# A Fourier mixing kernel rewritten: d folded at its centre, 32-row inverse tiles, PSUM bank by bank, the exchange in two ways

## The chip, the cores and the metric

One core of one Trainium2 chip. The metric is device time in microseconds (us) of one execution. The executions of one kernel spread here over about 3%, so each run is given as a median with its range, and a run that is 1.5% above the fastest of its kernel counts as "slow" and is left out of the ratios. Every ratio below is the mean time of one kernel's fast runs over that of the kernel before's fast runs in the same rounds, so it is not quite the ratio of the medians beside it. Where two variants are compared, the means of their fast runs are used; the changed kernel's is 153.7 us.

## The reference, cut to what matters

```python
g = sigmoid((x * gate_w).sum(-1, keepdims=True))      # x: (1, 2048, 1024) bf16
a = irfft2(rfft2(x) * (A_w_r + 1j * A_w_i))           # over (2048, 1024), fp32, then bf16
b = irfft2(rfft2(x) * (B_w_r + 1j * B_w_i))
return g * a + (1 - g) * b
```

The transforms are matmuls with cosine and sine tables. The 2048 rows are split as 16 x 128: F1 transforms over 128, F2 over d, F3 over the remaining 16 with the twiddles; then come the products with the weights A and B; then the inverse: I1 (16), I2 (128, with the gate folded into its table), I3 (d). The frequencies make sixteen "units", eight even and eight odd. Each unit's I1 output, 128 partitions by 2048 bf16 (0.52 MB), has to change places before I2: what lies across partitions must lie along a row. This is the *exchange*, from the tile `rl` to the row tiles `Re` (even) and `Ro` (odd), which are 32 KB per partition each. I2 of a half can't start before all eight units of the half have been exchanged.

## The kernel before

```python
    pp = ctx.enter_context(tc.tile_pool(name="pp", bufs=3, space=bass.MemoryType.PSUM))   # three buffers of two banks
    ...
    def i1(n, r):
        ...
        if r == 0:
            RLs[n] = wk.tile([P, 2, 2, 512], BF16, name="rl", tag="rl", bufs=4)
        rl = RLs[n]
        nc.scalar.copy(out=rl[:, :, r, :], in_=ps[:].rearrange("p (t m) -> p t m", t=2))
        if r == 1:
            for tt in range(2):
                t = 2 * u + tt
                p0 = 32 * (t // 4) + t % 4
                nc.gpsimd.dma_start(RR[par][p0:p0 + 29:4, :, :], rl[:, tt].rearrange("p r m -> p (r m)"))
    ...
    for n in range(12):
        f2(n)
        ...
        if n >= 3:
            i1(n - 3, 0)
        if n >= 1:
            f3(n - 1)
        if n >= 3:
            i1(n - 3, 1)
        if n >= 1:
            cmul(n - 1)          # two products and two sums on VectorE
        if n == 2:
            gate_z()
```

Two transfers of 256 KB per unit go through the GpSimd queue.

Of the kernel before, what the change touches and what calls it, by code (L numbers as in the profile page):

```python
# [20 lines left out]
WID = (257, 256)  # L21
PIT = (258, 256)
# [25 lines left out]

def make_constants():
# [3 lines left out]
    E = np.zeros((NT, 2, 2, 2, 128))  # L53
    EZ = np.zeros((NT, 2, 2, 2, 128))
    for t in range(NT):
        for j, k2 in enumerate(quad_reps(t)):
            th = 2 * np.pi * s2 * k2 / 128
            F[:, t, j // 2, 0, j % 2] = np.cos(th)
            F[:, t, j // 2, 1, j % 2] = -np.sin(th)
            E[t, j // 2, 0, j % 2] = np.cos(th)  # L60
            E[t, j // 2, 1, j % 2] = np.sin(th)
            EZ[t, j // 2, 0, j % 2] = 2 * np.cos(th)
            EZ[t, j // 2, 1, j % 2] = -2 * np.sin(th)
            if k2 == 0:
                F[:, t, j // 2, 1, j % 2] = np.cos(np.pi * s2)
                E[t, j // 2, 1, j % 2] = np.cos(np.pi * s2)
                EZ[t, j // 2, 0, j % 2] = 1
                EZ[t, j // 2, 1, j % 2] = np.cos(np.pi * s2)
    F = F.reshape(128, 128)
    c["F1"] = _bf16np(np.concatenate([F, -F], axis=1))  # L70
    c["E"] = _bf16np(E.reshape(4, 4, 8, 128).transpose(0, 2, 1, 3).reshape(128, 128))
    c["EZ"] = _bf16np(EZ.reshape(128, 128) / 128)
    d1 = np.arange(512)
    i = np.arange(256)
    FD = np.zeros((512, 2, 2, 256))
    IG = np.zeros((2, 2, 256, 512))
    for eo in range(2):
        m = 2 * i + eo
        ph = 2 * np.pi * np.outer(d1, m) / D
        FD[:, eo, 0] = np.cos(ph)  # L80
        IG[eo, 0] = 2 * np.cos(ph).T
        if eo == 0:
            IG[0, 0, 0] = 1
        m = 2 * i + (2 if eo == 0 else 1)
        ph = 2 * np.pi * np.outer(d1, m) / D
        FD[:, eo, 1] = -np.sin(ph)
        IG[eo, 1] = -2 * np.sin(ph).T
        if eo == 0:
            FD[:, 0, 1, 255] = np.cos(np.pi * d1)
            IG[0, 1, 255] = np.cos(np.pi * d1)  # L90
    IG /= S * D
    c["FD"] = _bf16np(FD.reshape(4, 128, 2, 512).transpose(1, 2, 0, 3))
    c["IG"] = _bf16np(IG.reshape(2, 2, 2, 128, 512).transpose(3, 0, 1, 2, 4).reshape(128, 8, 512))
    s1 = np.arange(NS1)
    WF = np.zeros((128, NT, 3, 64))
    WI = np.zeros((128, NT, 3, 64))
    for t in range(NT):
        for jh in range(2):
# [4 lines left out]
            for p in range(64):  # L103
                w = np.exp(-2j * np.pi * k[p] * s1 / S)
                kk = k[p] % 128
                if kk in (0, 64):
                    cc = 0 if kk == 0 else 1
                    al[:, cc, 0, p] = w
                    be[cc, 0, :, p] = w.conj()
                    continue  # L110
                eps = 1 if kk in reps else -1
                j = reps.index(kk if eps > 0 else 128 - kk)
                al[:, 0, j, p] = w
                al[:, 1, j, p] = 1j * eps * w
                be[0, j, :, p] = w.conj()
                be[1, j, :, p] = 1j * eps * w.conj()
            al = al.reshape(64, 64)
            be = be.reshape(64, 64).T
            h = slice(64 * jh, 64 * jh + 64)
            WF[h, t, 0], WF[h, t, 1], WF[h, t, 2] = al.real, al.imag, -al.imag  # L120
            h = h if t % 2 == 0 else slice(64 - 64 * jh, 128 - 64 * jh)
            WI[h, t, 0], WI[h, t, 1], WI[h, t, 2] = be.real, be.imag, -be.imag
    c["WF"] = _bf16np(WF)
    c["WI"] = _bf16np(WI)
# [4 lines left out]
def gated_mix(ctx, tc, x_in, we_in, wo_in, gw_in, out):  # L129
# [3 lines left out]
    xv = x_in.flatten_outer_dims().rearrange("(s2 s1) d -> s2 s1 d", s1=NS1)  # L133
# [5 lines left out]
    wp = ctx.enter_context(tc.tile_pool(name="wp", bufs=1))  # L139
    wk = ctx.enter_context(tc.tile_pool(name="wk", bufs=2))  # L140
    pp = ctx.enter_context(tc.tile_pool(name="pp", bufs=3, space=bass.MemoryType.PSUM))
    pl_pool = tc.alloc_tile_pool(name="plp", bufs=1, space=bass.MemoryType.PSUM)
# [4 lines left out]
    def ptile():  # L147
        return pp.tile([P, 1024], F32, name="pt", tag="pt")

    ctx.enter_context(tc.manual_schedule())  # L150
    warm = const.tile([P, 512], BF16, name="warm")
    nc.vector.memset(warm[:], 0.0)
    wps = ptile()
    for _ in range(6):
        nc.tensor.matmul(wps[:, 0:512], lhsT=warm[:, 0:128], rhs=warm[:], start=True, stop=True)  # L155
    F1 = const.tile([P, 2, 128], BF16, name="f1")
    nc.scalar.dma_start(F1[:].rearrange("p a b -> p (a b)"), dr["F1"])
    gws = const.tile([P, 8], BF16, name="gws")
    nc.scalar.dma_start(gws[:], gw_in)
    Re = big.tile([P, 16 * 1024], BF16, name="re")  # L160
    Ro = big.tile([P, 16 * 1024], BF16, name="ro")
    x = Re[:].rearrange("p (s d) -> p s d", s=NS1)
    for s0, n in ((0, 1), (1, 1), (2, 2), (4, 2), (6, 2), (8, 2), (10, 2), (12, 2), (14, 2)):
        nc.sync.dma_start(x[:, s0:s0 + n, :], xv[:, s0:s0 + n, :])
    FD = const.tile([P, 2, 4, 512], BF16, name="fd")
    WF = const.tile([P, NT, 3, 64], BF16, name="wf")
    WI = const.tile([P, NT, 3, 64], BF16, name="wi")
    IG = const.tile([P, 8, 512], BF16, name="ig")
    Ec = const.tile([P, 128], BF16, name="ec")
    Ez = const.tile([P, 128], BF16, name="ez")  # L170

    y = big.tile([P, 4, 2, 2 * NT, NS1, 4], BF16, name="y")
    Ws = {}
    wt = [wp.tile([P, 2064], BF16, name=f"w{k}", tag=f"w{k}") for k in range(4)]

    def load_w(n):
        par, u = n // NU, n % NU
        if n < 4 or 8 <= n < 12:
            w = wt[n % 4][:]
        elif n < 8:  # L180
            w = Ro[:, (n - 4) * 2064:(n - 3) * 2064]
        else:
            w = y[:, n - 12, 0].rearrange("p t s c -> p (t s c)")
        w = w[:, 0:8 * PIT[par]].rearrange("p (t a m) -> p t a m", t=2, a=4)
        nc.sync.dma_start(w, w_in[par][u])
        Ws[n] = w

    nc.sync.dma_start(FD[:, 0], dr["FD"][:, 0])
    nc.sync.dma_start(WF[:, 0:4], dr["WF"][:, 0:4])
    load_w(0)  # L190
    nc.sync.dma_start(Ez[:], dr["EZ"])
    nc.sync.dma_start(WI[:, 0:4], dr["WI"][:, 0:4])
    load_w(1)
    nc.sync.dma_start(WF[:, 4:16], dr["WF"][:, 4:16])
    load_w(2)
    nc.sync.dma_start(WI[:, 4:16], dr["WI"][:, 4:16])
    nc.sync.dma_start(Ec[:], dr["E"])
    for n in range(3, 8):
        load_w(n)
    nc.sync.dma_start(FD[:, 1], dr["FD"][:, 1])  # L200
    nc.sync.dma_start(IG[:], dr["IG"])

    gwz = const.tile([P, 8, 32], BF16, name="gwz")
    nc.gpsimd.memset(gwz[:], 0.0)
    gh = const.tile([P, 8], F32, name="gh")
    junk = const.tile([P, 8], F32, name="junk")
    nc.scalar.activation(junk[:], gwz[:, 0, 0:8], ACT.Sigmoid)
    nc.vector.tensor_scalar(gh[:], gws[:], 0.5, None, ALU.mult)
    gq = gwz[:].rearrange("p (q e) c -> p q e c", e=2)
    nc.vector.tensor_tensor(gq[:, :, 0, 0], gh[:, 0:4], gh[:, 4:8], ALU.add)  # L210
    nc.vector.tensor_tensor(gq[:, :, 1, 0], gh[:, 0:4], gh[:, 4:8], ALU.subtract)

    yo = y[:].rearrange("p q e t s c -> p (q e t) s c")
    for s1 in range(NS1):
        ps = ptile()
        for q in range(4):
            for h in range(2):
                nc.tensor.matmul(ps[:, q * 256:(q + 1) * 256],  # L218
                                 lhsT=x[:, s1, h * 512 + q * 128:h * 512 + (q + 1) * 128],
                                 rhs=(bc(F1[:, 0, :]).to_broadcast([P, 2, 128]) if h == 0 else F1[:]), start=(h == 0), stop=(h == 1))  # L220
        i_ = ps[:].rearrange("p (a c) -> p a c", c=4)
        if s1 == 15:
            for e, cp in ((0, nc.scalar.copy), (1, nc.vector.tensor_copy)):
                cp(out=y[:, :, e, :, s1, :], in_=ps[:].rearrange("p (q e t c) -> p q e t c", q=4, e=2, c=4)[:, :, e])
        elif s1 % 2 == 1:
            nc.vector.tensor_copy(out=yo[:, :, s1, :], in_=i_)  # L226
        else:
            nc.scalar.copy(out=yo[:, :, s1, :], in_=i_)  # L228

    RR = [r[:].rearrange("p (s f) -> p s f", s=NS1) for r in (Re, Ro)]  # L230
    EV = Re[:].bitcast(F32).rearrange("p (s f) -> p s f", s=NS1)
    EA = const.tile([P, NS1, 128], BF16, name="ea")
    EB = const.tile([P, NS1, 128], BF16, name="eb")
    zt = const.tile([P, NS1], BF16, name="zt")

    def gate_hat():
        ps = ptile()
        for e in range(2):
            for q in range(4):
# [154 lines left out]
    for n in range(12):  # L394
        f2(n)
        if n == 0:
            gate_hat()
# [89 lines left out]
```

## Time and profile before

146.2 us median (144.8 to 148.8); its profile spans 144.4 us. The span falls into five stretches: to the first F2 matmul, to the first product, to the first I2 of the even half, to the first I2 of the odd half, to the end. These are two, from a table of stretches of the kernel before (us from and to; length; busy time of each engine with its instructions; granted clock; DMA share; GB/s):

```profile
core 0: us, PE busy (x) PEld busy (x) DVE busy (x) ACT busy (x) POOL busy (x), PEclk, DMA share, GB/s
...
29.60:76.60 47.00, 38.21 (x427) 18.16 (x433) 42.28 (x54) 40.80 (x44) 10.81 (x18) 0.93 0.81 221
76.60:114.90 38.30, 34.22 (x346) 18.25 (x353) 24.01 (x30) 28.77 (x31) 8.29 (x14) 1.00 0.41 103
```

The transfers of the exchange, from the part on DMA issues (KB each, median us from issue to landing):

```profile
re<-rl POOLq DMA_DIRECT2D x16, 256.0 KB, 8.0
ro<-rl POOLq DMA_DIRECT2D x16, 256.0 KB, 5.1
```

### The profile page before, as it was taken

The numbers are of one execution on the slowest core, as the hardware profiler recorded it, in microseconds if no ns is written. First come the engines' busy times: TensorE is split into PE (matmuls) and PEld (weight loads), VectorE is DVE, ScalarE is ACT, GpSimd is POOL, SyncE is SP. The second block draws the span as 40 slices with busy tenths as digits, with TensorE's granted clock in tenths as the row PEclk, the third lists the DMA queues.
The fourth block names the chain that finished last, engine by engine and source line by source line (L and its number), as shares of the span: only waits on it lengthen the run. The fifth ranks groups of instructions, "written<-read, shape, count | busy, mean of one in ns | idle before, by whom it ended". The sixth has DMA issues, their size and how long they took to land.

```text
span 144.4 us, 2878 instructions
## 1 busy us (share of the span) xinstructions
PE 121.9 (84%) x1188; PEld 68.1 (47%) x1206; DVE 97.6 (68%) x113; ACT 93.3 (65%) x97; POOL 19.6 (14%) x37
## 2 busy tenths in 40 slices
PE   6999979929899898888867999868869999999910
PEld 2688844416344443334324345433455665756500
DVE  0177740089279999999999279599433456898990
ACT  4255546665699999999995899997935244253200
POOL 1000000000033222233333033033330000000000
PEclk9999999975799999999999999999999999999985
DMA  4999999968716999999865315527464000464553
GB/s 148 298 361 419 406 411 405 415 244 284 297 14 168 240 279 278 353 250 202 163 139 133 126 18 140 131 43 168 110 166 110 0 0 0 167 253 166 208 228 145
DMA packets 11088, 29.19 MB, mean 202 GB/s; under 512 B 3781, under 2 KB 4165, under 8 KB 10949
## 3 DMA queue, kind: packets, MB, share of 16 engines
q1 hardware_dynamic: 6048, 20.55, 38.3%
q0 software_dynamic: 4608, 8.41, 24.8%
q8 instruction: 9, 0.15, 0.5%
q10 hardware_dynamic: 420, 0.07, 0.3%
q14 instruction: 3, 0.02, 0.0%
HBM read 16.42 MB, written 4.19 MB: 143 GB/s over the span
## 4 chain that ended last, share of the span: by engine, by line
PE 55%; ACT 24%; DMA 9%; issue 4%; DVE 2%; another core or an unknown queue 2%; DVEq 1%; POOL 0%; ACTq 0%; POOLq 0%
PE pt L378 18%; PE pt L218 10%; PE pt L275 10%; ACT rl L349 10%; PE pv L367 9%; DMA re<-rl 5%; DMA zt<-zs 4%; ACT X L310 4%; ACT T L279 3%; PE pt L344 3%; ACT V L370 2%; PE pt L155 2%; ACT zs L245 2%; DVE ot L390 2%
## 5 line engine op out<-in xcount | busy, mean ns | idle before, releaser
L275 PE MATMUL pt<-fd,y 128*128 128x512 bf16 x117 | 30.5, 394 | 3.8 <-ACT rl L349 2.6
L349 ACT CAST rl<-pt 128x1024 bf16<-128x1024 f32 x32 | 32.9, 1038 | 0.0
L378 PE MATMUL pt<-ig,V 128*128 128x512 bf16 x121 | 29.6, 379 | 1.1 <-ACT V L370 0.7
L370 ACT CAST V<-pv 128x1024 bf16<-128x1024 f32 x16 | 16.3, 1021 | 19.2 <-PE pv L367 19.2
L344 PE MATMUL pt<-Y,wi 64*64 64x512 bf16 x256 | 20.1, 387 | 3.8 <-ACT T L279 0.8
L275 PEld LDWEIGHTS <-y 128*128 128x128 bf16 x128 | 12.6, 100 | 20.3 <-issue 8.6
L279 ACT CAST T<-pt 128x1024 bf16<-128x1024 f32 x16 | 16.3, 1017 | 8.3 <-PE pt L275 4.1
L378 PEld LDWEIGHTS <-V 128*128 128x128 bf16 x128 | 11.7, 98 | 13.9 <-ACT V L370 1.9
L354 POOL DMA_DIRECT2D re<-rl x16 | 9.6, 606 | 59.8 <-ACT rl L349 59.8
L310 ACT CAST X<-pt 128x1024 bf16<-128x1024 f32 x16 | 16.5, 1033 | 0.0
L218 PE MATMUL pt<-f_84,re 128*128 128x256 bf16 x128 | 15.6, 289 | 0.0
L218 PEld LDWEIGHTS <-re 128*128 128x128 bf16 x128 | 13.0, 103 | 3.1 <-DMA re<-in_x_dram 0.8
L228 ACT CAST y<-pt 128x1024 bf16<-128x1024 f32 x8 | 8.1, 1013 | 8.4 <-PE pt L218 8.4
L354 POOL DMA_DIRECT2D ro<-rl x16 | 9.5, 596 | 26.4 <-ACT rl L349 26.4
L386 DVE COPY re<-pt 128x1024 f32<-128x1024 f32 x5 | 6.1, 1225 | 10.2 <-PE pt L378 10.2
L226 DVE CAST y<-pt 128x1024 bf16<-128x1024 f32 x7 | 8.6, 1225 | 5.2 <-PE pt L218 5.2
L344 PEld LDWEIGHTS <-wi 64*64 64x64 bf16 x256 | 6.4, 106 | 11.9 <-issue 10.7
L389 DVE TENSOR_TENSOR ot<-pt,re 128x1024 bf16<-128x1024 f32 x8 | 9.8, 1224 | 3.0 <-PE pt L378 3.0
L367 PE MATMUL pv<-ea,re 128*128 128x128 bf16 x64 | 8.1, 219 | 2.9 <-DMA re<-rl 1.7
L295 PE MATMUL pt<-T,wf 64*64 64x512 bf16 (+2 forms) x192 | 9.8, 307 | 0.4 <-ACT T L279 0.3
L367 PEld LDWEIGHTS <-re 128*128 128x128 bf16 x128 | 7.5, 98 | 5.4 <-issue 2.5
L390 DVE TENSOR_TENSOR ot<-re,pt 128x1024 bf16<-128x1024 f32 x8 | 9.7, 1210 | 0.0
(96 smaller groups left out, 128.2 us busy)
## 6 DMA issues: line engine op xcount, KB each, us to landing
re<-rl POOLq DMA_DIRECT2D x16, 256.0 KB, 8.0
ro<-rl POOLq DMA_DIRECT2D x16, 256.0 KB, 5.1
out_dram<-ot SPq DMA_DIRECT2D x8, 512.0 KB, 2.6
re<-in_x_dram SPq DMA_DIRECT2D x7, 512.0 KB, 8.6
ro<-in_we_dram SPq DMA_DIRECT2D x4, 516.0 KB, 8.0
y<-in_wo_dram SPq DMA_DIRECT2D x4, 512.0 KB, 6.5
fd<-cst_fd SPq DMA_DIRECT2D x2, 512.0 KB, 9.1
ig<-cst_ig SPq DMA_DIRECT2D x1, 1024.0 KB
```

The costliest lines, as they stand in the source:

```text
L218: nc.tensor.matmul(ps[:, q * 256:(q + 1) * 256], lhsT=x[:, s1, h * 512 + q * 128:h * 512 + (q + 1) * 128], rhs=(bc(F1[:, 0, :]).to_broadca ...
L275: nc.tensor.matmul(ps[:, tt * 512:(tt + 1) * 512], lhsT=y[:, q, par, 2 * t:2 * t + 2, :, :].rearrange("p j s c -> p (j s c)"), rhs=FD[:, p ...
L279: nc.scalar.copy(out=T[:].rearrange("p a b -> p (a b)"), in_=ps[:])
L295: nc.tensor.matmul(ps[ho, tt * 512 + dst:tt * 512 + dst + ln], lhsT=WF[hp(jh), 2 * u + tt, w, :], rhs=T[hp(jh), tt, src:src + ln], start=( ...
L310: nc.scalar.copy(out=xo, in_=ps[:].rearrange("p (t r m) -> p t r m", t=2, r=2))
L344: nc.tensor.matmul(ps[hp(jh), tt * 512:(tt + 1) * 512], lhsT=WI[hin, 2 * u + tt, w, :], rhs=Y[hin, k, 2 * tt:2 * tt + 2, o:o + 256], start ...
L349: nc.scalar.copy(out=rl[:, :, r, :], in_=ps[:].rearrange("p (t m) -> p t m", t=2))
L354: nc.gpsimd.dma_start(RR[par][p0:p0 + 29:4, :, :], rl[:, tt].rearrange("p r m -> p (r m)"))
L367: nc.tensor.matmul(ps[:, s * 512 + ch * 128:s * 512 + ch * 128 + 128], lhsT=RR[par][:, s1, c0 + 256 * ab:c0 + 256 * ab + 128], rhs=Ew[:, s ...
L370: nc.scalar.copy(out=V[:].rearrange("p s c k -> p (s c k)"), in_=ps[:])
L378: nc.tensor.matmul(ps[:, s * 512:(s + 1) * 512], lhsT=V[:, s, ch, :], rhs=IG[:, par * 4 + ch, :], start=(ch == 0), stop=(ch == 3))
L390: nc.vector.tensor_tensor(ot[:, :, 1, :], ev, pv, ALU.subtract)
```

## The change

Its intent: less work on TensorE and VectorE, PSUM given out bank by bank instead of in three buffers of two, every instruction placed by a list. Folding d at its half-sample centre halves F2 and part of I3; I1 multiplies the products directly in 32-row tiles, so VectorE's sums go; units 0, 2, 4, ... are exchanged by the GpSimd queue, units 1, 3, 5, ... by a store to DRAM and a reload on the sync queue. The diff of some 1,000 lines, cut to its core:

```diff
+ORDER = """
+warm:6 c:A:F1 c:A:gws tab:A x:S:0:1 x:S:1:1 ...
+F2:5:0:0 P:2:0 N:0:P ... HS:1:S J:0:4:6
+W:S:6 T:4:0:A T:5:1:A W:S:7 ... c:S:IG ... HL:1:S ... H:2:0:P ...
+"""                                 # (cut: 537 entries in all)
-    pp = ctx.enter_context(tc.tile_pool(name="pp", bufs=3, space=bass.MemoryType.PSUM))
+    pp = ctx.enter_context(tc.tile_pool(name="pp", bufs=1, space=bass.MemoryType.PSUM))
+    psum = pp.tile([P, 4096], F32, name="ps")
+def exchange_row(t, i):
+    u = t // 2
+    return 64 * (u // 4) + 32 * (t % 2) + 16 * (i % 2) + 4 * (i // 2) + u % 4
-            for q in range(4):       # F2: four matmuls of 512 columns
-                nc.tensor.matmul(ps[:, tt * 512:(tt + 1) * 512], ...
+        for v in range(2):           # F2: four of 256
+            for b in range(2):
+                nc.tensor.matmul(ps[:, v * 256:v * 256 + 256], ...
-        nc.vector.tensor_tensor(Y[:, 0, :, 0:M], p1[:, :, 0, 0:M], p2[:, :, 1, 0:M], ALU.subtract)
-        nc.vector.tensor_tensor(Y[:, 1, :, 0:M], p1[:, :, 1, 0:M], p2[:, :, 0, 0:M], ALU.add)
+        for q, (w, ri, wi, a, b) in enumerate(mm):      # I1: the sums inside PSUM, K = 32
+            ...
+                        nc.tensor.matmul(o[:, :, a:b], lhsT=lh, rhs=src[r, ri, wi, tt, :, a:b], start=(q % 4 == 0), stop=(q % 4 == 3))
-                nc.gpsimd.dma_start(RR[par][p0:p0 + 29:4, :, :], rl[:, tt].rearrange("p r m -> p (r m)"))
+    def shuffle(n, tt, q):                              # H
+        p0 = exchange_row(2 * u + tt, 0)
+        for j in range(2):
+            Q[q].dma_start((Re, Ro)[par][p0 + 16 * j:p0 + 16 * j + 13:4, :], rl[:, tt, j, :])
+    def scratch_store(n, q):                            # HS
+        SC[n] = dm.tile([16, 16384], BF16, name=f"sc{n}", tag=f"sc{n}")
+        Q[q].dma_start(SC[n][:].rearrange("(a c) (f m) -> (c f) a m", a=4, m=512), RLs[n][:].rearrange("p t j m -> p (t j) m"))
+    def scratch_load(n, q):                             # HL
+        p0 = exchange_row(2 * (n % NU), 0)
+        Q[q].dma_start((Re, Ro)[n // NU][p0:p0 + 61:4, :], SC[n][:])
```

## The prediction

> **What bounds the kernel now.** I read the busy shares first, then a table of stretches, then the chain of waits, then durations of single instructions.
>
> ```profile
> PE 121.9 (84%) x1188; PEld 68.1 (47%) x1206; DVE 97.6 (68%) x113; ACT 93.3 (65%) x97; POOL 19.6 (14%) x37
> ```
>
> No engine is full over the whole span, so the stages have different limits. I cut the span where the chain changes: start, forward transform over s2 (F1), gate, twelve-odd units of middle work, inverse over s2 and d, tail.
>
> ```profile
> core 0: us, PE busy (x) PEld busy (x) DVE busy (x) ACT busy (x) POOL busy (x), PEclk, DMA share, GB/s
> 0.00:3.79 3.79, 2.60 (x6) 0.74 (x6) 0.27 (x1) 1.49 (x2) 0.51 (x5) 1.00 0.53 157
> 3.79:20.14 16.35, 15.64 (x129) 12.99 (x128) 9.01 (x11) 8.59 (x9) 0.00 (x0) 1.00 1.00 376
> 20.14:37.39 17.25, 13.68 (x117) 6.76 (x121) 8.30 (x11) 9.06 (x8) 0.00 (x0) 0.81 0.90 347
> 37.39:96.30 58.91, 51.54 (x592) 24.35 (x600) 48.93 (x61) 54.46 (x59) 15.54 (x26) 1.00 0.67 173
> 96.30:136.10 39.80, 36.77 (x338) 22.67 (x346) 26.47 (x27) 19.68 (x21) 3.55 (x6) 1.00 0.38 119
> 136.10:144.40 8.30, 1.69 (x8) 0.59 (x6) 4.61 (x4) 0.00 (x0) 0.00 (x0) 0.73 0.46 190
> ```
>
> F1 and the inverse are PE's (15.64 of 16.35, 36.77 of 39.80). The gate stretch belongs to nobody: PE 13.68 of 17.25 at a clock of 0.81, ACT half idle. The middle is ACT's (54.46 of 58.91). The tail of 8.30 is two DVE pairs and a store.
>
> ```profile
> 26.32 5.80 DMA zt<-zs
> ...
> 43.49 0.38 PE pt L275
> 43.86 0.05 issue
> 43.92 1.47 PE pt L275 x6
> 45.39 0.02 issue
> 45.41 0.02 ACTq L279
> 45.43 0.04 issue
> 45.47 0.95 ACT T L279
> 46.42 0.97 ACT rl L349
> ...
> 117.72 0.89 PE pv L367 x16
> 118.62 1.73 PE pt L378 x8
> ```
>
> The chain shows a wait of 5.80 us for the small gate transfer, then a ring in the middle: eight 512-column matmuls (1.9), the T copy (0.95), an rl copy (0.97), and the next matmuls. T copies start at 41.51 and 45.47, so one unit costs 3.96 us. Four copies of 1024 columns start 0.905 apart (3.62 a unit), hence ACT alone is not quite the bound; the three PSUM buffers of two banks, shared by both, add the rest. DVE is close too: two products at 1.15 and two sums at about 0.61 and 0.69 are 3.6. At 117.72 PE is gapless, at 0.89 + 1.73 = 2.62 per step.
>
> ```profile
> L349 ACT CAST rl<-pt 128x1024 bf16<-128x1024 f32 x32 | 32.9, 1038 | 0.0
> L224 DVE CAST y<-pt 128x512 bf16<-128x512 f32 x1 | 0.7, 693 | 1.2 <-ACT y L224 1.2
> L224 ACT CAST y<-pt 128x512 bf16<-128x512 f32 x1 | 0.6, 592 | 0.0
> ```
>
> Halving a copy does not halve it: ACT 1038 against 592, DVE 1225 against 693. Successive starts lie about 0.1 closer than the durations, so my prices on the path are ACT 0.905 / 0.49 / 0.275 us and DVE 1.15 / 0.61 / 0.35 us for 1024 / 512 / 256 columns (the last by the same line, an estimate).
>
> [...]weight loads hidden: 0.89 / 16 = 56 ns and 1.73 / 8 = 216 ns; F1 at 256 columns gives 1.76 us per 16, 110 ns.[...]
>
> **The change, part by part.**
> PE, from the counts of the order list. F1: 28 half tiles of eight 128-column matmuls and 4 of eight 256-column ones, 224 x 0.056 + 32 x 0.110 = 16.0 (now 128 x 0.110 = 14.1): +1.9. Folding d at its centre makes cosine and sine act on separate halves, so F2 is 128 matmuls of 256 columns: 14.1 against 27.7, -13.6. F3 stays at 16 x 0.46 = 7.4, and the 64 one-column extras go (-1). I1 now takes the four products directly, K=32: four passes over eight tiles. Today eight 64x64 matmuls (two passes) take 0.56 us in the chain, so four passes should be 1.12 per unit, the same as today's, plus sixteen tiny matmuls at some 0.025 in the eight even units (0.4): 16 x 1.12 + 8 x 0.4 = 21.1 against 17.9, +3.2. I2 stays at 256 x 0.056 = 14.3. I3: 72 x 0.216 + 56 x 0.110 = 21.7 against 27.7, -6.0. Gate 3, warm-up 3.8. Sum 101 against some 115 at the same prices.
> DVE. The 32 sums that made Y go: 32 x about 0.64 = -20.5. The 32 products stay (36.8). Added: 16 folds of two 256-column operations (11.2), 10 even sums of two (7.0), a quarter of the rl copies (8 x 1.15 = 9.2), 11 V copies (6.7), 6 T copies (3.7). The old F1 copies (8.7) go, and the sixteen final 1024-column operations (18.4) become 16 + 4 of 512 and two sums on SBUF (13.4). Total 97 against some 92.
> ACT. rl 24 x 0.905, T 26 x 0.49, X 15 x 0.905, V 21 x 0.49, F1 copies 10.1, the rest some 11: 79 against 88.
> [...]
> Exchange. Today an rl transfer lands after 8.0 (re) and 5.1 us (ro). Half now makes two hops through DRAM, at least two of the 2.6 us that a 512 KB store takes now. It adds 4.2 MB written and read, but the early load (about 16 MB) is unchanged; DMA share in the middle was 0.67.
> PSUM by single banks and the gate moved eight units later take away the ring and the 5.80 us wait.
>
> Which engine is heaviest in each section of the list, by those prices (PE / DVE / ACT):
> - to the first F2: 17.6 / 12.6 / 9.1
> - to the first product: 6.2 / 5.3 / 5.2
> - to the first I2 of the even half: 34.8 / 38.8 / 38.0
> - to the first I2 of the odd half: 22.4 / 19.6 / 18.5
> - to the end: 20.1 / 20.5 / 8.1
>
> The maxima sum to 105.5. Add 1.2 before the first matmul, about 2 for DVE's late start in the last section and about 3 for the last store: 112, if each section's heaviest engine never waited. The same sum for the kernel before is 1.2 + 16.8 + 62 (ACT, 20 to 96 us) + 36.8 + 8.3 = 125, and it ran 144.4 in the profile: 19 us, or 15%, of waiting. About 8 of those are the gate stretch and 4 to 5 the ring; the remaining 6 or 7 are the ordinary kind. The new kernel has closer loads on three engines and many more dependencies, so I give it 6 to 10 us of waiting: 118 to 122, and take 121.
>
> **The rivals.**
> (a) The DRAM hop becomes the new wait. The last even unit's store and reload must finish within some 9 to 11 us of other work; today the first I2 already waited 1.7 us for its transfer. Loads queued behind a waiting store on the sync queue could starve a product. For it: 0.99 DMA share in the 57 to 73 us stretch. Against: the list puts at least ten PE operations between. It would give 126 to 132.
> (b) Small instructions eat the gain: I1's 32 to 48 matmuls per unit could be limited by issue, not by columns. Each matmul then costs 45 ns rather than 35: 32 x 10 ns x 16 units = 5 us more, much of it under DVE: 124.
> (c) DVE becomes the bound[...]: only four folds meet products, but if products slow by a fifth this is 7 us: 127.
> (d) The list fits the chip perfectly: 113 to 115.
> (e) The change falls flat, as in-order queues on four engines hold each other up as badly as before: 112 x 1.15 = 129, still faster.
>
> **Range and chances.** Rivals (a) to (c) put 124 to 132 above the centre and (d) 113 below; I take 121, range 114 to 130. A slowdown would need over 34 us of new waits on top of 112, and nothing in the profile has that size. Faster by over 2%: 0.95; within 2%: 0.03; slower: 0.02.
>
> **What would show it.** F2's matmuls at 256 columns, busy near 14; DVE near 105 busy and above 80% of the span; ACT below 90; no T-to-T period of 3.96 but about 3.2; no long wait for zt; the inverse stretch still PE's; a tail under 6 us after the last matmul. It is wrong if the first I2 waits over 3 us for re or ro, if I1 takes over 1.5 us a unit in the odd half, or if DVE's products grow past 1.24 us.

## The result, and the profile after

155.0 us median (153.1 to 157.2; the mean of the fast runs is 153.7), against 146.2 before: ratio 1.052, interval 1.040 to 1.064. The kernel is slower, where 121 us and "faster" had been predicted. The busy line of the changed kernel's page (its profiled run was slow, at a mean granted clock of 0.886; the later-gate variant below has the same stretches within 3.2 us):

```profile
PE 115.2 (74%) x1819; PEld 78.0 (50%) x1819; DVE 100.3 (65%) x153; ACT 85.0 (55%) x135; POOL 69.1 (44%) x99
```

TensorE has less to do than before (115.2 against 121.9, although at a lower clock, 0.886 against 0.961), ScalarE too; nobody is above 75%. So the time went into waiting. The same stretches as above, of the changed kernel:

```profile
22.80:27.20 4.40, 4.40 (x64) 3.12 (x62) 3.21 (x6) 3.27 (x6) 4.24 (x14) 1.00 1.00 397
27.20:88.00 60.80, 41.94 (x951) 26.48 (x948) 41.79 (x40) 40.41 (x55) 27.53 (x36) 0.89 0.81 216
88.00:127.30 39.30, 28.05 (x377) 18.63 (x378) 20.51 (x34) 21.23 (x33) 8.21 (x12) 0.78 0.59 161
127.30:155.40 28.10, 20.32 (x194) 13.11 (x191) 22.17 (x39) 8.87 (x17) 17.76 (x14) 0.91 0.38 151
```

The first two and the last stretch cost together 22.8 + 4.4 + 28.1 = 55.3 us, near the 50.5 that the prediction's parts make for them (17.6 + 1.2, 6.2, 20.5 + 2 + 3). The two middle ones cost 100.1 where 61.2 had been predicted, and no compute engine is busy for more than 42 of 60.8 and 28 of 39.3 us. What they look like in slices of 3.9 us:

```profile
PE   6799999998997309997056206999607999999900
...
PEclk9999999999999955999759955799995699999985
DMA  5999999407989987937989831699875400064555
```

Four slices in the middle have a zero for PE, and TensorE's clock is granted at about half (5) in or after them. In three of the four the DMA engines are busy (8, 9, 3 and 7 tenths). What the engines waited for (engine, tile and line <- releaser: us in total, times, longest):

```profile
ACT rl L220 <- DMA sc<-rl: 27.4, 5, 9.3
...
DVE rl L222 <- DMA sc<-rl: 15.8, 2, 10.6
...
PE ps L429 <- DMA zt<-zs: 5.5, 1, 5.5
...
SPq L544 <- DVE rl L222: 38.2, 4, 13.3
```

The copies of I1's output into `rl` wait for a buffer, because the scratch store out of that buffer hasn't landed. There are four such buffers. Once a copy waits, PSUM stays full and PE stops behind it (6.5 us once for a copy on ScalarE, 5.8 us in two waits for copies on VectorE). The gate's little transfer is still waited for (5.5 us), and the sync queue stands 38 us behind evictions with loads behind it: it issued nothing from 45.2 to 58.6 us, then the store that it had waited for and three loads by 61.2. One of the holes as it ends, in the timeline (start, length, then at the end in brackets the idle time before and who ended it):

```profile
57.31 1.01 ACT L220 CAST rl<-ps 128x1024 bf16<-128x1024 f32 x1 [5.57 <-DMA sc<-rl]
57.33 1.22 DVE L222 CAST rl<-ps 128x1024 bf16<-128x1024 f32 x1 [5.16 <-DMA sc<-rl]
```

And the transfers (compare 8.0 and 5.1 before):

```profile
sc<-rl SPq DMA_DIRECT2D x8, 512.0 KB, 5.9
...
re<-sc SPq DMA_DIRECT2D x4, 512.0 KB, 12.0
...
re<-rl POOLq DMA_DIRECT2D x16, 128.0 KB, 9.1
```

A unit through scratch takes 5.9 + 12.0 us (6.8 for a reload into `Ro`). But late landings may be a cause or a consequence, and four explanations fit: the order of the queues, too few buffers, the DMA engines' total, or a pace of the exchange of its own. They were told apart on the chip.

### The profile page after: what moved, and what is told of

Its sections match the earlier page's. It is cut to its first block, busy times and chain, and to the rows that moved or that the text cites.

```text
span 155.4 us, 4366 instructions
## 1 busy us (share of the span) xinstructions
PE 115.2 (74%) x1819; PEld 78.0 (50%) x1819; DVE 100.3 (65%) x153; ACT 85.0 (55%) x135; POOL 69.1 (44%) x99
## 5 line engine op out<-in xcount | busy, mean ns | idle before, releaser
L220 ACT CAST rl<-ps 128x1024 bf16<-128x1024 f32 x24 | 24.1, 1036 | 29.5 <-DMA sc<-rl 27.4
L524 PE MATMUL ps<-p,wj 32*64 32x510 bf16 (+2 forms) x768 | 21.2, 321 | 7.8 <-DVE rl L222 5.8
L220 ACT COPY wx<-ps 128x512 f32<-128x512 f32 (+1 forms) x34 | 15.1, 490 | 18.1 <-PE ps L343 8.8
L391 POOL TENSOR_TENSOR y<-wx 128x256 bf16<-128x256 f32 x24 | 19.9, 850 | 6.8 <-ACT wx L220 6.8
L222 DVE CAST rl<-ps 128x1024 bf16<-128x1024 f32 x8 | 9.7, 1219 | 17.7 <-DMA sc<-rl 15.8
L496 DVE TENSOR_TENSOR p<-X,ro 128x2048 bf16<-128x2048 bf16 x16 | 20.2, 1304 | 1.0 <-ACT X L220 0.9
L615 POOL TENSOR_TENSOR ot<-re,wx 128x512 bf16<-128x512 f32 x12 | 14.9, 1272 | 12.6 <-ACT wx L220 12.2
L449 PE MATMUL ps<-fd,y 128*128 128x256 bf16 x128 | 18.3, 291 | 1.0 <-ACT rl L220 0.8
L575 PE MATMUL ps<-ig,V 128*128 128x512 bf16 x72 | 18.1, 393 | 0.0
L220 ACT CAST X<-ps 128x1024 bf16<-128x1024 f32 x15 | 15.6, 1039 | 3.5 <-PE ps L482 1.9
L539 POOL DMA_DIRECT2D re<-rl x16 | 11.2, 704 | 11.3 <-ACT rl L220 11.1
L482 PE MATMUL ps<-T,wf 64*64 64x510 bf16 (+3 forms) x128 | 11.2, 364 | 6.5 <-ACT rl L220 6.5
L343 PE MATMUL ps<-f,re 128*128 128x128 bf16 x224 | 14.9, 232 | 0.8 <-DMA re<-in_x_dram 0.8
```

The lines of the kernel that those rows point to most:

```text
L220: nc.scalar.copy(out=out, in_=in_)
L222: Q[e].tensor_copy(out=out, in_=in_)
L343: nc.tensor.matmul(o, lhsT=lh, rhs=rh, start=(h == 0), stop=(h == 1))
L391: Q[e].tensor_tensor(yo[:, v, k:k + n, s1, :], a.rearrange("p (k c) -> p k c", c=4), b.rearrange("p (k c) -> p k c", c=4), op)
L449: nc.tensor.matmul(ps[:, v * 256:v * 256 + 256], lhsT=y[:, v, par, b, 2 * t:2 * t + 2, :, :].rearrange("p j s c -> p (j s c)"), rhs=C["FD" ...
L482: nc.tensor.matmul(view(ps[ho, tt * 512:(tt + 1) * 512], dst), lhsT=lh, rhs=view(T[hp(jh), tt, :], src), start=(g == 2), stop=(w in ("s", 1)))
```

## The experiments

All are edits of the changed kernel unless said. In the diffs, tokens are those of the list: H sends by GpSimd (P), sync (S) or ScalarE's (A) queue, HS stores to scratch, HL reloads.

### First four: order, scratch, pool

**A fixed ring of buffers.** The allocator had given the four `rl` buffers out unevenly: by the reading of the compiled addresses, unit 5 got the buffer of unit 3, unit 6 that of 5.

```diff
-            RLs[n] = wk.tile([P, 2, 2, 512], BF16, name="rl", tag="rl", bufs=RLB)
+            RLs[n] = wk.tile([P, 2, 2, 512], BF16, name="rl", tag=f"rl{len(RLs) % RLB}", bufs=1)   # also for ot
```

> Only the reuse of the four rl buffers changes: a fixed ring of four in place of the order that the allocator chose (there ten of sixteen units take over the buffer of a unit whose DRAM store has just been issued). Theory A (the eviction of a unit waits for the landing of a recent unit's DRAM store, because buffers are handed on too early): the three idle stretches of 5.3, 6.2 and 9.5 us shrink to a third, 134 to 141 us. Rival B (the DMA engines are simply too full; a later unit waits just as long): within 2% of 155. Rival C (the kernel's engines are slower than priced and the waits only fill slack): within 2% of 155.

Measured: 151.8 us (151.2 to 153.3), ratio 1.043 (1.033 to 1.053). By the fast runs 152.0 against 153.7, and the intervals of the two ratios overlap: far from the 134 to 141 of theory A. Copies now waited for other landings: "ACT rl <- DMA re<-rl" 20.0 us. The allocation is at most a small fault, not the cause.

**No scratch.** HS and HL are dropped; the result is wrong.

> Wrong result on purpose: the store to DRAM and the reload of the eight odd-numbered units are left out, all else stays. Theory A and rival B both: 120 to 128 us, as the prediction had it for the rest. Rival C: still 140 or more, with PE, DVE or ACT full where the idle stretches were.

Measured: 133.2 us (132.3 to 133.8), ratio 0.913 (0.906 to 0.921). Some 21 us go with the scratch half (fast runs): between the 120 to 128 of theory A and rival B and the 140 of rival C. The one long wait left on TensorE is for the gate's transfer, 10.0 us.

**All by the GpSimd queue.** `HS:n:S` becomes `H:n:0:P H:n:1:P`, HL goes.

> All sixteen units exchanged by GpSimd's queue, no DRAM hop. GpSimd issues 32 more transfers (0.69 us each, 22 us more of its time). Theory A: 130 to 138, since buffers still come free only after a landing of 6 to 9 us. Rival B: 126 to 132, as 8.3 MB of DRAM traffic goes and 4.2 MB of on-chip traffic comes. If GpSimd's own queue is the bound: 150 or more.

Measured: 150.7 us (149.5 to 151.8), ratio 1.036 (1.028 to 1.044). Without any scratch hop it is still slower than before. Of the expectations only the last fits, GpSimd's own queue as the bound. This was the first hint that it isn't scratch as such.

**Stores from ScalarE's queue.** `HS:n:S` becomes `HS:n:A`.

> The eight stores to DRAM are issued from ScalarE's queue in place of the sync queue, the reloads stay. If the stores are late because they stand behind loads and waiting reloads in the sync queue (a part of theory A): they land in 4 to 5 us, 138 to 146 us. If the DMA engines are full whatever the queue (rival B): 150 to 157.

Measured: 155.0 us (153.1 to 157.1), ratio 1.055 (1.044 to 1.066): no gain, as rival B had it. The longest wait for a store fell from 9.3 to 6.7 us, but their sum was still 22 us on ScalarE (27 before).

### Second four: the gate, and fewer loads

**The gate later.** The two gate matmul groups, their sigmoids and the first gate weights move 6 to 9 us down the list.

```diff
-... P:7:1 F3:8:6 GZ:0:2 R:5:0:D ... GS:0 ... GZ:1:4 ... GW:D:0 GS:1 ... GW:D:4 ...
+... F3:11:4 GZ:0:2 ... R:7:1:A GS:0 ... R:8:0:D GW:D:0 R:8:1:A GZ:1:2 ... R:9:0:A GS:1 ... P:13:0 GW:D:4 ...
```

> The changed kernel with only the gate matmuls, sigmoids and first weights placed two to three units (6 to 9 us) later, so that no engine stands behind the gate's little transfer. Theory (DMA engines full; any wait taken away comes back at the next late landing): the 5.5 us wait for zt goes, but the time stays within 2% of 155, 151 to 157, as the same transfers must still land. Rival (the gate wait is a cost of its own): 5 us or more less, 150 or below.

Measured: 151.9 us (150.6 to 152.8), ratio 1.043 (1.031 to 1.055). The result was wrong: GZ:0 took PSUM bank 2 before unit 7's output had been read from it. The same instructions ran, so the time may be read, with that caution; the later runs have it mended. By the fast runs (151.8 against 153.7) some 2 us of the 5.5 came back, and the intervals of the two ratios overlap; the theory's range holds. Its profile gives the stretches 22.4, 4.3, 57.6, 38.6 and 28.1 us.

**The gate later and no scratch** (wrong).

> Wrong result on purpose: no scratch stores and loads (as in the run of 133 us), and the gate later. With the scratch traffic gone the 10 us wait for zt was the one large wait left. Theory (compute was priced right, the transfers were not in the prediction's sum): 118 to 125, near the predicted 121, PE waiting under 2 us for any landing. Rival (small matmuls and partial fits cost more than priced, whatever the transfers do): 128 to 133.

Measured: 131.0 us (129.3 to 131.8), ratio 0.894 (0.880 to 0.907). By its number this is the rival. But the middle stretch (50.6 us) still had waits for landings of 5.7 (VectorE) and 4.0 us (ScalarE), so the run doesn't tell small matmuls from transfers; the run with no exchange at all, below, does.

**All by the GpSimd queue, ring, gate later.**

> All sixteen units through the GpSimd queue, the four exchange buffers in fixed turn, and the gate later; a right result. It has some 9 us less DMA-engine time than the changed kernel. Theory (DMA total decides): 143 to 149, about the time of the kernel before, with waits of 5 us or more for exchange landings left. Rival (each of the three was an order fault that added up): 138 or less.

Measured: 154.0 us (153.3 to 154.6), ratio 1.058 (1.050 to 1.067), with the same wrong result. Both expectations missed. Mended order gave no gain over the plain GpSimd variant: order isn't the cause.

**Seven weight loads fewer** (wrong): all odd units read unit 8's weights.

```diff
+        if n > 8:
+            Ws[n] = wx[:, 0].rearrange("p (t a m) -> p t a m", t=2, a=4)
+            return
```

> Wrong result on purpose: the changed kernel, scratch and all, but the weight tiles of units 9 to 15 aren't loaded (all odd units read unit 8's), which takes 3.7 MB or 9 to 10 us of all DMA engines' time out of the middle. Theory (DMA engines full): 9 us or more less, 140 to 146. Rival (it is the latency of the hop through DRAM, store then load, with four buffers, not the volume): within 2% of 155.

Measured: 149.4 us (148.3 to 150.6), ratio 1.025 (1.013 to 1.036). By the fast runs 4.7 us less (149.0 against 153.7) for 9 to 10 us of DMA time (an estimate: 3.7 MB at the 397 GB/s of the stretch before): the loads share in it, but neither expectation holds.

### Third four: compute alone, order again, buffers

**No exchange at all** (wrong; H, HS and HL dropped, gate later).

> Wrong result on purpose: no exchange transfers at all (neither the scratch hop nor the GpSimd queue), the gate placed later as before but with its PSUM bank taken only after it is read (the two earlier late-gate runs overwrote unit 7's bank, hence their wrong results). This is the compute alone with its loads. Theory (compute was priced about right): 117 to 124, and the middle stretch, first product to first even I2, takes 40 to 43 us instead of the 50.6 that it still took with half the exchange. Rival (compute itself was mispriced): 127 or more with the middle at 48 or above.

Measured: 124.4 us (124.1 to 126.2); by the fast runs 124.6 beside 144.8 of the kernel before. Its two middle stretches:

```profile
26.30:72.90 46.60, 40.62 (x951) 26.46 (x950) 41.56 (x40) 40.47 (x56) 14.35 (x16) 0.96 0.42 161
72.90:96.00 23.10, 22.58 (x376) 15.72 (x377) 20.54 (x35) 20.91 (x33) 0.00 (x0) 1.00 0.01 1
```

The compute, loads and all, takes 124 us; the total is a little over the predicted 121, the middle (46.6) between the theory's 40 to 43 and the rival's 48. In the odd half PE is busy for 22.58 of 23.10 us, against 22.4 predicted. The fair partner is the later-gate kernel, as the gate was moved here too: 151.8 less 124.6 (fast runs) makes some 27 us that are the exchange's doing. The prices of the instructions didn't make the kernel slower.

**Loads first.** Ring, gate later (mended), and the loads `W:6`, `W:7`, `IG` ahead of the first scratch store.

> Scratch and all, a right result: fixed ring of four exchange buffers, later gate, and the loads of two weight tiles and of the last table are issued ahead of the first scratch store, so that the sync queue no longer stands 13 us behind an eviction with 1.8 MB of loads behind it. Theory (order: idle DMA engines early, a backlog later): 141 to 147. Rival (the number of exchange buffers against an 8 to 12 us landing bounds the middle, whatever the order): 149 to 152, as with the ring alone.

Measured: 152.5 us (150.0 to 154.2), a right result; 150.5 by the fast runs. The rival. Order falls for good.

**Six buffers, all by the GpSimd queue**, on top of this: `PB, RLB, VB = 3, 4, 2` becomes `2, 6, 2`.

> All units through the GpSimd queue, loads first, later gate, six exchange buffers in turn instead of four (and two product buffers instead of three, to make room); a right result. Theory (buffers against landing time): 138 to 145, waits for exchange landings under 10 us in sum. Rival (the GpSimd queue itself is too slow, some 2.5 us of all engines per unit beside the loads): 148 to 154 as with four.

Measured: 151.5 us (151.0 to 156.0), right; 151.3 by the fast runs. Again the rival.

**Six buffers with the scratch half.**

> As the loads-first kernel with the scratch hop, with six exchange buffers and two product buffers; a right result. Theory (buffers against landing time): 5 us or more below the loads-first run of the same call. Rival (DMA time or order bounds): within 2% of that run.

Measured: 150.7 us (150.2 to 153.3), right; 150.5 by the fast runs, as the loads-first run. The rival. The ring, the order and the buffers together are worth some 1% (ratios to the kernel before 1.039 by the fast runs, against 1.052). What is left is the rate at which the exchange can go at all.

### The exchange by itself

**Bench 1.** The kernel's setup with all compute replaced by phases of eight units each (4.2 MB), each phase fenced by VectorE copies that read what was written. Zeros out, wrong.

```diff
+    for u in range(8):                       # 1: the form of the kernel before
+        form_before(u, "P")
+    fence()
+    for u in range(8):                       # 2: the form of the changed kernel
+        form_after(u, "P")
+    fence()
+    for u in range(8): scratch_store(u, "S") # 3: the scratch hop
+    for u in range(8): scratch_load(u, "S")
+    ...                                      # 4: form 2 by the sync queue; 5: with loads; 6: half and half
```

> No computation (zeros out, wrong on purpose): six phases, each sending eight units (4.2 MB) from SBUF to SBUF rows, fenced by copies that read what was written. Phase 1: GpSimd queue, the form of the kernel before (two transfers of 256 KB a unit, 2 KB pieces); 2: GpSimd queue, the changed form (four of 128 KB, 1 KB pieces); 3: all scratch stores, then all scratch loads; 4: the changed form straight from the sync queue; 5: phase 2 with eight weight loads beside it; 6: half GpSimd queue, half sync queue. Theory (each way has a pace, and the changed form's on the GpSimd queue is slow): phase 2 takes 30 us or more (3.8 or more per unit), phase 1 below 24, phase 3 some 32, phase 4 below 20. Rival (the pace is only that of the packets on 16 engines): phases 1 and 2 both about 20 us.

Measured, phases 1 to 3 as stretches (from and to; length; VectorE, GpSimd; clock; DMA share; GB/s):

```profile
15.70:40.80 25.10, 0.01 (x1) 9.62 (x16) 1.00 0.86 167
42.80:76.50 33.70, 0.00 (x0) 21.86 (x32) 1.00 0.57 126
77.00:111.90 34.90, 1.23 (x7) 0.00 (x0) 1.00 0.95 240
```

Phase 1 came a little above the 24 expected. This is the row that the prediction lacked. Eight units cost 25.1 us in the old form (3.1 a unit), 33.7 in the changed form (4.2), 34.9 by scratch (4.4). The compute alone got 26 of the 32 products, that is 13 units, done in the 46.6 us of its middle stretch: a unit every 3.6 us. Note the share: the scratch hop fills the DMA engines (0.95), while the changed form is slow with engines 43% idle. Phase 4 took about 50 us, where below 20 was expected: direct transfers from the sync queue are slower still. Phases 5 and 6 are blurred (phase 5's loads had run ahead into phase 4) but for one reading: half by GpSimd and half directly by the sync queue took 40.9 us.

**Direct transfers from the sync queue**, as the way out: `HS:n:S` becomes `H:n:0:S H:n:1:S` on the loads-first kernel.

> The loads-first kernel (ring, later gate) with the scratch store and reload replaced by four direct transfers per unit from the sync queue; a right result. Theory (pace of the path): 134 to 142. Rival (all that is exchanged costs alike, whatever the path): 147 to 152.

Measured: 155.4 us (154.5 to 156.5), ratio 1.079 (1.053 to 1.104), right. Both expectations missed; the bench offers the reason: at 40.9 us for eight units this is the slowest pair of ways.

**All directly by the sync queue.**

> All sixteen units by direct transfers from the sync queue, nothing by GpSimd; a right result. Theory (pace of the path): 130 to 142, at or below the half-and-half run. Rival: 147 or more.

Measured: 180.4 us (179.5 to 180.5), ratio 1.248 (1.231 to 1.265), right. The theory as put was wrong about which way is fast, but the run is the strongest sign that the pace of the exchange sets the time: nothing else differs from the loads-first kernel, and by the fast runs it is some 30 us slower (180.2 against 150.5). Its two middle stretches:

```profile
26.90:100.60 73.70, 43.48 (x952) 27.38 (x950) 42.82 (x41) 41.05 (x56) 14.34 (x16) 0.79 0.50 155
100.60:148.40 47.80, 26.57 (x379) 18.20 (x377) 20.66 (x36) 20.59 (x33) 0.00 (x0) 0.84 0.27 90
```

**Bench 2.** Half and half as the changed kernel sends; three quarters and one quarter; and the old rows in 1 KB pieces.

```diff
+    for u in range(0, 8, 2):                 # 1
+        form_after(u, "P"); scratch_store(u + 1, "S")
+    for u in range(0, 8, 2): scratch_load(u + 1, "S")
+    ...                                      # 2: six by GpSimd, two by scratch
+            for r in range(2):               # 3: eight rows, pieces of 1 KB instead of 2
+                Q[q].dma_start(R3[p0:p0 + 29:4, :, 512 * r:512 * r + 512], rl[:, tt, r, :])
```

> No computation (zeros out, wrong on purpose): three fenced phases of eight units each. Phase 1: four units by GpSimd queue and four by scratch at the same time, as the changed kernel sends; 2: six by GpSimd queue and two by scratch; 3: the rows of the kernel before, but in 1 KB pieces (four transfers of 128 KB a unit). Theory: the ways share the 16 engines, whose time for four and four is 9.6 + 16.5 us, so phase 1 takes 26 to 30 us (3.3 to 3.7 a unit), not the 17 of two independent halves; phase 2 25 to 28; phase 3, if the piece size is the cause, 32 to 36 as the changed form took (33.7). Rival: phase 3 at the 25 us of the old form, so that the row pattern and not the piece is the cause.

Measured: 35.5, 35.9 and 25.2 us. The first and the third phase, with the columns of bench 1:

```profile
15.40:50.90 35.50, 0.01 (x1) 11.10 (x16) 1.00 0.79 177
...
90.40:115.60 25.20, 0.11 (x1) 18.93 (x32) 1.00 0.76 167
```

Two surprises. Sending half each way gives nothing: 4.4 us a unit, as slow as either way alone (the estimates of 26 to 30 and 25 to 28 from engine time were wrong). And the pieces are innocent: with eight rows, 1 KB pieces are as quick as the old form (25.2 against 25.1).

**The kernel before with its exchange in 1 KB pieces.** This puts the form that phase 3 measured into the old schedule:

```diff
-                nc.gpsimd.dma_start(RR[par][p0:p0 + 29:4, :, :], rl[:, tt].rearrange("p r m -> p (r m)"))
+                for rr in range(2):
+                    nc.gpsimd.dma_start(RR[par][p0:p0 + 29:4, :, 512 * rr:512 * rr + 512], rl[:, tt, rr, :])
```

> The kernel before with one part of the change alone, the form of the exchange: each of its two 256 KB transfers per unit is sent as two of 128 KB in 1 KB pieces, still by the GpSimd queue; a right result. Its units come 3.96 us apart. Theory (the pace of the exchange binds a whole kernel where it exceeds what the units need): 4.2 us per unit is a little over 3.96, so 147 to 153, with exchange landings of 8 us or more and waits of rl copies on them. Rival (old schedule has room enough): within 1% of 146.

Measured: 146.9 us, ratio 1.001 (0.994 to 1.008), right. The expected 4.2 us per unit wasn't the pace of this form, as bench 2 showed; with the pace unchanged the time is unchanged.

**Bench 3: rows per transfer.** Same sources, same 128 KB, same 1 KB pieces; 4, 8 or 16 destination rows; first by the GpSimd queue, then by the sync queue.

```diff
+                if n == 4:   d = Re[p0:p0 + 13:4, :]
+                elif n == 8: d = Re[p0:p0 + 29:4, 8192 * j:8192 * j + 8192]
+                else:        d = Re[p0:p0 + 61:4, c:c + 4096]
+                Q[q].dma_start(d, rl[:, tt, j, :])
```

> No computation (zeros out, wrong on purpose): six fenced phases of eight units each, all of 128 KB transfers in 1 KB pieces, with 4, 8 and 16 destination rows per transfer, first by the GpSimd queue, then by the sync queue. Theory (one transfer runs on as many engines as it has destination rows, up to 16): GpSimd queue about 34, 25 and 20 us; sync queue about 46, 24 and under 20 us, each halving while the engines bind. Rival[...]: 16 rows as slow as 8, about 25 and 24. If 4 and 8 rows differ by under 10%, both fall.

Measured, with the columns of bench 1:

```profile
15.10:50.60 35.50, 0.00 (x0) 22.12 (x32) 1.00 0.55 120
52.40:77.50 25.10, 0.00 (x0) 18.95 (x32) 1.00 0.75 168
79.40:101.20 21.80, 0.32 (x2) 16.68 (x32) 1.00 0.91 192
102.70:151.00 48.30, 0.01 (x1) 0.00 (x0) 1.00 0.26 87
152.70:178.80 26.10, 0.32 (x2) 0.00 (x0) 1.00 0.49 161
180.40:202.30 21.90, 0.29 (x1) 0.00 (x0) 1.00 0.70 192
```

On the sync queue the share of the 16 engines that is busy is 0.26 with 4 rows, 0.49 with 8 and 0.70 with 16, that is 4.2, 7.8 and 11.2 engines in the mean. The time falls from 48.3 to 26.1 to 21.9 us. For 4 and 8 rows this is near the theory's one engine per row; for 16 it falls short. By the GpSimd queue the same transfers keep 8.8, 12.0 and 14.6 engines busy and take 35.5, 25.1 and 21.8 us, so four rows cost most there too, but the sync queue suffers more (48.3 against 35.5). Why the two queues differ for the same rows isn't shown by these runs. The rival made 16 rows as slow as 8; they are 3 to 4 us quicker on both queues, so it falls. A second rival is that four rows simply give the engines more work. But on the GpSimd queue time x share x 16 comes to 312, 301 and 317 us of engine time (an estimate from the lines above): the engines don't work longer for four rows, fewer of them work at once.

## Why the prediction was wrong, point by point

**The step that failed** is "Exchange": it priced the landing of one transfer ("Half now makes two hops through DRAM, at least two of the 2.6 us") and never the pace of sixteen. The table of sections has rows for PE, DVE and ACT and none for the exchange, and "the early load is unchanged; DMA share in the middle was 0.67" was left standing as if a share were kept when the stretch gets shorter. The missing term, from the benches, for the two middle stretches: the first unit leaves 7.6 us after the first product (27.2 to 34.8 in the changed kernel); sixteen units at 35.5 us per eight take 71; the loads left in these stretches are ten weight tiles and a table, 6.0 MB, 15 us at the 397 GB/s of the stretch before. If they are simply added (an estimate, made after the runs) it makes 94 us, against 61.2 in the prediction. The same sum for every way of sending, beside the two stretches measured ("slow": the profiled run was of that state):

| variant | eight units, us | estimate, us | measured, us |
|---|---|---|---|
| no exchange | 0 | compute: 61.2 predicted | 69.7 |
| half, GpSimd only (gate later) | 33.7 for all it sends | 56, so compute: 69.7 | 74.3 (slow) |
| all by GpSimd; with ring and later gate; six buffers | 33.7 | 90 | 92.8; 94.6; 96.6 (slow) |
| changed kernel; gate later; stores from ScalarE's queue | 35.5 | 94 | 100.1 (slow); 96.2; 96.0 |
| ring; loads first; six buffers | 35.5 | 94 | 94.5; 97.1 (slow); 92.2 |
| half by GpSimd, half direct | 40.9 | 104 | 97.1 |
| all direct | 48.3 | 119 | 121.5 |

The sum follows the chip within some 7 us, but most rows lie close together; what carries it are its two ends, GpSimd's half alone and all direct. And there is one exception: with 3.7 MB of loads taken out it says 84 where 93.0 were measured, so loads and exchange are not simply additive. The kernel before fits: 12.0 us until its first unit leaves, two times 25.1 for the exchange and 15 for its 5.8 MB of loads make 77, its two stretches last 85.3, so there the exchange was hidden. The change shortened the compute in these stretches to 70 us and raised the sum from 77 to 94: it crossed over.

**Compute.** Right in sum: 124.4 us without exchange against 121. Section by section, predicted and then measured in that run: 18.8 and 22.0 to the first F2, 6.2 and 4.3, 38.8 and 46.6 in the middle, 22.4 and 23.1 in the even half's inverse, 25.5 and 27.8 at the end. The middle was planned too full: DVE was busy for 41.6 of its 46.6 us. Slips in the working were small: its DVE parts add up to 95.6, not 97, PE's before to 117, not 115, ACT's 62 is 63.5 in the trace, and the even units have 32 tiny matmuls in I1, not sixteen.

**"A slowdown would need over 34 us of new waits on top of 112, and nothing in the profile has that size."** It had: some 27 us came from a stream that had been hidden, and the profile of before couldn't show it as a wait. Some of it may be amplified: in or after each hole TensorE's clock was granted at about half (5 in the slices), and F2's matmuls took 291 ns in the mean against 273 in the no-exchange run (the slowest 421, in the later-gate run too, against 284).

**Rivals.** (a), the DRAM hop as the new wait, had the right place and a wrong size and reason: 126 to 132, as a latency to be hidden. Without the hop, all by GpSimd, the kernel still took 150.7. (b) fell: I1 takes 20.8 us busy for 768 matmuls in the no-exchange run, 1.3 a unit with the small ones of the even half. (c), products slowed by GpSimd's folds, is real but small. In the changed kernel a fold on GpSimd took 0.73 us (median), and three of the 24 met a product and took 1.70 to 1.74. The products of that time, on weights in `Ro`, took 1304 ns in the mean and up to 1750 (1303 and 1748 in the no-exchange run), those later 1215 to 1217: some 16 x 86 ns = 1.4 us in all. (d) didn't come. (e) was right that the kernel would fall flat, but held queue order for the reason, and mended order brought about 1%.

**The gate.** "PSUM by single banks and the gate moved eight units later take away ... the 5.80 us wait": the wait was still 5.5 us, and 10 us in the no-scratch run; while the small transfer was under way the DMA engines were full (share 1.01 from 46.7 to 58.4 us in the changed kernel). Moving it gave back 2 us at most.

**The tests it set itself.** F2 near 14: 16.5 in the no-exchange run, a little high. DVE near 105 busy and over 80%: 100.3 and 65%. ACT below 90: 85.0. A unit every 3.2 us or so: 3.6 in the no-exchange run. The inverse still PE's: there 22.58 of 23.10 us, in the changed kernel 28.05 of 39.3. A tail under 6 us after the last matmul: 7.8 (147.6 to 155.4). I1 over 1.5 us a unit in the odd half: no, 9.7 us for eight. DVE's products past 1.24 us: yes on the weights in `Ro`, but in the no-exchange run too, so that isn't the slowdown. "Wrong if the first I2 waits over 3 us for re or ro": in the changed kernel the odd half's first I2 waited 3.8 us for ro. This test came true (1.5 us in the later-gate run), but it is the small end of the matter; the 27.4 and 15.8 us before `rl` were not among the tests. GpSimd's operations took 0.73 us per 256 columns where no product met them and 1.27 per 512, off the path here.

**What stays open.** No variant of the changed kernel with a right result beat the kernel before (the best took 150.3 to 150.5 us by the fast runs). The exchange was taken out and slowed down, but never made faster in the changed kernel, and the number of rows was varied only in benches of one execution each. Why half and half add up instead of overlapping isn't settled: the scratch hop alone has the engines at 0.95, the pair at 0.79. Also open is whether the changed kernel can be given eight or more rows per transfer; its I1 leaves four rows in each 128-partition piece. By the sum above an exchange at bench 3's 16-row pace (21.8 us) would need 66 us and be just hidden, but this wasn't run.

## What to carry to other kernels

Give every stream that runs beside the compute its own row in the section table: bytes, or better units, times a measured pace, and when the compute gets faster ask at which point the hidden stream becomes the path. Read the access pattern of each transfer as a cost: here four destination rows instead of eight, at the same bytes and pieces, took 35.5 us instead of 25.1 in the bench. And if mending order and buffers gives 1%, stop mending, take the stream out, and then measure it by itself.
